# Keeping the first group's turned attention rows in their ring places instead of writing them to DRAM and reading them back

## The chip, the cores and the metric

The kernel runs on one core of a Trainium2 chip. The metric is the device time of one execution in microseconds (us); times of several executions are given with their median. A profile of one execution gives every instruction's start and duration on the engines: TensorE (PE, with its weight loads as PEld), VectorE (DVE), ScalarE (ACT), GpSimd (POOL), and SyncE (SP), whose queue issues nearly all transfers.

## The reference

Three layers on 2304 tokens of 512 channels, in float32. A windowed attention (4 batches of 576 positions, 8 heads of 64, each position sees itself and the 127 before it, with a slope by head); a dense layer with h - tanh(h); and a mixture of 8 experts, in which each token goes to the one expert whose embedding it is most like.

```python
scores = scale * q @ k^T + slope * -(distance), masked to 0 <= distance < 128
attn = softmax(scores) @ v                        # -> x [2304, 512]
h = x @ w_in                                      # w_in [512, 2048]
x = (h - tanh(h)) @ w_out                         # w_out [2048, 512]
e = argmax(norm(x) @ norm(expert_emb)^T / tau);  gate = softmax(...)[e]
out = gate * (relu(x @ w1[e]) @ w2[e])            # w1 [8, 512, 1024], w2 [8, 1024, 512]
```

## The kernel before

The tokens are 18 blocks of 128; two blocks are a group, so there are 9 groups. Products are split into a high and a low part (hi, lo), and three products of the parts make one.

Attention makes a block in four quarters (two heads of scores at a time): scores on TensorE (L463, L469), the bias and the row maximum on VectorE, exp on ScalarE, then the split of the probabilities (L510, L515), a transposing transfer issued by SP (L520, tile pt), the product with the values on TensorE (L551), and a sum into the block's rows xr (L570). xr is a single tile. `x_out` turns it on TensorE (four transposes, L642), copies the high part into the tile xT on ScalarE (L654) and subtracts for the low part on VectorE (L655). xT is a ring of four places, two for a group.

The dense layer takes a group in 8 steps. In a step, two half steps of 12 matmuls each make h from xT and w_in (L695), ScalarE and VectorE make g = h - tanh(h) and its split (L700, L703, L708, tile gl at L712), and four quarters of three matmuls each add g times w_out into the group's accumulators acc (L719), one for each of its two blocks. There is only one pair of accumulators. Half of group 0's weights are not there yet at the start, so the order of visits is: group 0 with the first 4 of the 8 steps (its sums are spilled to DRAM, tile pa, `spill`), group 1 with all 8, group 0 with the other 4, and then groups 2 to 8. The steps are counted through over the visits, from 0 to 71: group 1 has steps 4 to 11, group 0's second visit steps 12 to 15, group 2 begins with step 16.

`route` is the gate of a group: the sums are copied from acc into the tile x2row (group 0: the spilled sums are reloaded into it, L755, and acc added, L759), squared and rooted, split three times (copies L793, subtractions L798, on the engine that the planner chooses), turned by a transfer (L802, x3T), multiplied by the embeddings for the logits (L807), and after the choice TensorE makes the positions (L848 to L851), GpSimd scatters both blocks into the experts' buckets in DRAM (L878). x2row is a single tile, so group 0's reload waits for group 1's scatters. Then the experts run.

What stands where is decided by a planner (`Plan`). Every piece of work is added with its engine (or a choice of engines) and its cost, a due time, and the names that it reads and writes; `order` gives each the engine and the place in that engine's queue at which it would start first by these costs. Each engine runs its queue in order. A piece that goes away can thus change the order of others.

In `x_out` before, the first two blocks are written to DRAM (px) from xr when they are made, and on group 0's second visit read back into xr and turned and split again. The ring places of both visits of group 0 are the same two, since the counter xi goes round by four:

```python
sl = [xi % XR, (xi + 1) % XR]      # XR = 4; visits 0, 1, 0 take places 0-1, 2-3, 0-1
```

Of the kernel before, what the change touches and what calls it, by code (L numbers as in the profile page):

```python
# [10 lines left out]
F32 = mybir.dt.float32  # L11
# [14 lines left out]
DM = H * D  # L26
# [19 lines left out]
N0 = 1  # L46
# [118 lines left out]
class Builder:  # L165
# [461 lines left out]
            P.add({"DVE": 0.5}, recip, due, r=["at"], w=sm)  # L627
            P.add({"DVE": 0.5, "POOL": 0.7}, mul, due, r=["at"] + sm, w=half)

    def x_out(self, P, b, s, due, back=False):  # L630

        nc = self.nc
        v = {}

        def reload(e):
            t = self.xr[b] = self.at.tile([128, DM], F32, tag="xr", name="xr", bufs=1)
            nc.sync.dma_start(out=t, in_=self.px[b])

        def tr(e):
            v["ps"] = self.misc()  # L640
            for k in range(KD):
                nc.tensor.transpose(v["ps"][:, k * 128:(k + 1) * 128], self.xr[b][:, k * 128:(k + 1) * 128],  # L642
                                    self.ident)

        pv = lambda: v["ps"].rearrange("p (k t) -> p k t", k=KD)
        hi, lo = [t[:, s] for t in self.xTs]
        xr, xt = [("xr", m) for m in range(4)], ("xT", s)
        if back:
            P.add({"SP": 0.73}, reload, due - 2, r=["at", ("px", b)], w=xr)
        elif b < 2 * N0:  # L650
            P.add({"SP": 0.73}, lambda e: nc.sync.dma_start(out=self.px[b], in_=self.xr[b]), due, r=["at"] + xr,
                  w=[("px", b)])
        P.add({"PE": 0.43}, tr, due, r=["at", "con"] + xr, w=[xt], take="misc")
        P.add({"ACT": 0.48}, lambda e: self.nc.scalar.copy(out=hi, in_=pv()), due, r=["at"], w=[xt])  # L654
        P.add({"DVE": 0.6}, lambda e: self.nc.vector.tensor_tensor(out=lo, in0=pv(), in1=hi.bitcast(F32),  # L655
                                                                   op=ALU.subtract), due, r=["at"], w=[xt],
              free="misc")
# [588 lines left out]
    def build(self):  # L1246
        tc, nc = self.tc, self.nc
        for n in ("kf", "qf", "vf", "sums", "oh4", "qst", "xr", "acc", "w"):
            setattr(self, n, {})
        self.setup()  # L1250
        dp = self.pool("dr", bufs=1, space=DRAM, tilewait=False)
        self.bucket = dp.tile([ROWS, ROW], F32, name="bucket")
        self.px = dp.tile([2 * N0, 128, DM], F32, name="px")
        self.pa = dp.tile([2 * N0, 128, DM], F32, name="pa")
        self.nw = 0
        P = Plan()
        P.add({"POOL": 0.6}, lambda e: self.small(), 0, w=["small", "cum"])
        self.zero(P)
        self.consts(P)
        self.small_loads(P, -9)  # L1260
        self.emb(P, -9)
        all_f = list(range(FP))
        fa, fb = all_f[:FA], all_f[FA:]
        visits = ([(g, fa) for g in range(N0)] + [(N0, all_f)] + [(g, fb) for g in range(N0)]
                  + [(g, all_f) for g in range(N0 + 1, NG)])

        def weights(fps, due, rate):
            for x, fp in enumerate(fps):
                for kind in "io":
                    for f in (2 * fp, 2 * fp + 1):  # L1270
                        self.weight(P, kind, f, due + x * rate + 1.2 * (kind == "o"))

        weights(fa, -WLEAD, WRATE)
        p, xi, seen = 0, 0, set()
        for g, fps in visits:
            sl = [xi % XR, (xi + 1) % XR]
            xi += 2
            rate = RATE if g <= N0 else 1.0
            for n in range(2):
                b = 2 * g + n  # L1280
                d0 = p - 8 * rate - LEAD + 4 * n * rate
                if g not in seen:
                    for hf in range(2):
                        due = d0 + 2 * hf * rate
                        self.qk_half(P, b, hf, due - QK)
                        if b < NF and hf == 0:
                            self.qk_early(P, b, due - QK - 2)
                            self.v_full(P, b, due)
                        if b >= NF - 1:
                            self.v_half(P, b, hf, due)  # L1290
                        for qq in range(2):
                            self.quarter(P, 4 * b + 2 * hf + qq, due + qq * rate)
                self.x_out(P, b, sl[n], -5 if g in seen else d0 + 4 * rate, g in seen)
            if g == N0:
                weights(fb, p + len(fa) - WLEAD2, WRATE2)
            for fp in fps:
                self.step(P, p, g, fp, sl, fp == fps[0], fp == fps[-1])
                for e in range(E):
                    if p == PAD + e // PADN:
                        self.pad(P, e, p)  # L1300
                p += 1
            if g < N0 and g not in seen:
                self.spill(P, p - 1, g, sl)
            else:
                if g == NG - 1:
                    self.moe2(P, p, lambda: self.route(P, g, sl, p))
                else:
                    self.route(P, g, sl, p + 1)
                if g == NG - 3:
                    self.choose(P, p + 2)  # L1310
            seen.add(g)
        with tc.manual_schedule():
            for fn, e in P.order({"misc": 1}):
                fn(e)
        self.overflow()
        while self.open:
            k = list(self.open)[-1]
            self.close(k)
# [183 lines left out]
```

## Time and profile before

| | |
|---|---|
| median of 3 runs | 810.32 us (808.01 to 810.85) |
| the profiled execution | 813.71 us, its span 812.0 us |
| TensorE busy | 775.1 us (95%), weight loads 684.4 us (84%) |
| VectorE, ScalarE, GpSimd busy | 569.6, 422.0, 227.1 us |
| moved by transfers | 118.90 MB, 146 GB/s on average |
| granted clock of TensorE, mean | 0.992 |

The span runs from the first to the last instruction. A busy share is an average over the whole span; what a stretch is worth is seen in that stretch alone.

### The profile page before, as it was taken

The numbers are of one execution on the slowest core, as the hardware profiler recorded it, in microseconds if no ns is written. First come the engines' busy times: TensorE is split into PE (matmuls) and PEld (weight loads), VectorE is DVE, ScalarE is ACT, GpSimd is POOL, SyncE is SP. The second block draws the span as 40 slices with busy tenths as digits, with TensorE's granted clock in tenths as the row PEclk, the third lists the DMA queues.
The fourth block names the chain that finished last, engine by engine and source line by source line (L and its number), as shares of the span: only waits on it lengthen the run. The fifth ranks groups of instructions, "written<-read, shape, count | busy, mean of one in ns | idle before, by whom it ended". The sixth has DMA issues, their size and how long they took to land. (4 is left out here: it accounts for less than half of the span.)

```text
span 812.0 us, 15246 instructions
## 1 busy us (share of the span) xinstructions
PE 775.1 (95%) x5225; PEld 684.4 (84%) x5225; DVE 569.6 (70%) x1544; ACT 422.0 (52%) x953; POOL 227.1 (28%) x242
## 2 busy tenths in 40 slices
PE   6999999988999998999999999989999999999995
PEld 4688998886888987888988989978879899989894
DVE  5788988968587697788787886776456665756420
ACT  4787866555354455555555643555246554545220
POOL 2113034646253145144242422321100211210210
PEclk9999999999999999999999999999999999999998
DMA  8896079666245335445364442474167666655100
GB/s 306 312 365 229 34 211 271 139 129 136 65 93 132 82 86 117 105 98 119 84 130 112 73 79 53 153 211 143 66 217 231 202 208 202 198 184 184 40 29 30
DMA packets 128264, 118.90 MB, mean 146 GB/s; under 512 B 87973, under 2 KB 92069, under 8 KB 128048
## 3 DMA queue, kind: packets, MB, share of 16 engines
q1 hardware_dynamic: 125152, 108.37, 48.7%
q0 software_dynamic: 3024, 9.46, 3.2%
q8 instruction: 43, 0.70, 0.4%
q14 instruction: 45, 0.37, 0.2%
HBM read 86.84 MB, written 17.08 MB: 128 GB/s over the span
## 5 line engine op out<-in xcount | busy, mean ns | idle before, releaser
L695 PE MATMUL h<-xT,wi 128*128 128x256 f32 x1728 | 225.5, 284 | 0.0
L695 PEld LDWEIGHTS h<-xT,wi 128*128 128x128 f32 x1728 | 217.0, 191 | 5.9 <-issue 1.3
L719 PE MATMUL acc<-wo,gh 128*128 128x512 f32 x576 | 184.8, 402 | 0.3 <-DVE x2row L759 0.3
L719 PE MATMUL acc<-wo,gl 128*128 128x512 f32 x288 | 113.8, 395 | 0.0
L719 PEld LDWEIGHTS acc<-wo,gh 128*128 128x128 f32 x576 | 100.0, 189 | 15.1 <-DVE x2row L759 0.5
L700 ACT ACTIVATE t<-h 128x512 f32<-128x512 f32 x72 | 43.1, 599 | 103.2 <-PE h L695 98.2
L1129 PE MATMUL y<-eo,ge 128*128 128x512 f32 x336 | 88.8, 399 | 0.5 <-ACT ge L1110 0.5
L505 ACT ACTIVATE p<-sc,mx 128x256 f32<-128x256 f32 (+1 forms) x128 | 59.3, 465 | 41.5 <-DVE mx L491 37.7
L1154 POOL DMA_INDIRECT out<-yo,ix x23 | 24.4, 1059 | 188.1 <-ACT yo L1150 39.8
L491 DVE CUSTOM_DVE_ANT_0 sc<-sc,bias 128x256 f32<-128x256 f32 (+1 forms) x144 | 52.6, 371 | 28.5 <-PE sc L469 19.6
L1129 PEld LDWEIGHTS y<-eo,ge 128*128 128x128 f32 x336 | 59.5, 188 | 10.8 <-ACT ge L1110 0.8
L712 DVE TENSOR_TENSOR gl<-t,gh 128x512 fp32r<-128x512 f32 x72 | 64.9, 902 | 4.9 <-ACT gh L708 4.3
L1027 DVE TENSOR_TENSOR eo<-est,eo 128x512 fp32r<-128x512 f32 x61 | 44.9, 738 | 28.8 <-ACT eo L1023 28.1
L719 PEld LDWEIGHTS acc<-wo,gl 128*128 128x128 f32 x288 | 54.4, 189 | 12.6 <-DVE gl L712 0.5
L1023 ACT CAST eo<-est 128x512 fp32r<-128x512 f32 x64 | 39.6, 620 | 37.1 <-PE y L1125 21.3
L1116 DVE SCALAR_TENSOR_TENSOR ge<-he,ge 128x256 fp32r<-128x256 f32 x104 | 28.7, 316 | 41.2 <-ACT ge L1110 41.2
L1094 PEld LDWEIGHTS he<-xA,ei 128*128 128x128 f32 x384 | 54.2, 188 | 2.5
L1094 PE MATMUL he<-xA,ei 128*128 128x288 f32 (+2 forms) x384 | 56.1, 295 | 0.0
L703 DVE TENSOR_TENSOR t<-h,t 128x512 f32<-128x512 f32 x72 | 49.4, 686 | 9.3 <-ACT t L700 9.1
L1110 ACT ACTIVATE ge<-he 128x288 fp32r<-128x288 f32 (+2 forms) x56 | 23.1, 415 | 62.9 <-PE he L1094 58.7
L1094 PEld LDWEIGHTS he<-xT,ei 128*128 128x128 f32 x384 | 53.4, 189 | 2.1
L1094 PE MATMUL he<-xT,ei 128*128 128x288 f32 (+2 forms) x384 | 54.8, 295 | 0.0
(202 smaller groups left out, 1312.1 us busy)
## 6 DMA issues: line engine op xcount, KB each, us to landing
est<-in_w SPq DMA_DIRECT2D x128, 256.0 KB, 3.2
rawi<-in_w_in SPq DMA_DIRECT2D x16, 511.8 KB, 6.9
rawo<-in_w_out SPq DMA_DIRECT2D x16, 511.8 KB, 5.0
stk<-in_k SPq DMA_DIRECT2D x30, 256.0 KB, 2.9
stq<-in_q SPq DMA_DIRECT2D x28, 256.0 KB, 3.1
bucket<-in_c_pad SPq DMA_DIRECT2D x8, 771.0 KB, 6.3
xe<-bucket SPq DMA_DIRECT2D x17, 257.0 KB, 3.5
vst<-in_v SPq DMA_DIRECT2D x30, 128.0 KB, 2.4
```

Source lines behind the costliest of these rows:

```text
L491: nc.vector.tensor_tensor_reduce(out=x, in0=x, in1=self.bias[:, h, c0:c1], scale=-0.125, scalar=mx[:, 1:2] if m else 3.0e38, op0=ALU.add, ...
L505: nc.scalar.activation(out=v["p32"][:, jj * W:(jj + 1) * W], in_=x, func=AF.Exp, scale=-1.0, bias=v["mx"][jj][:, 0:1], accum_out=self.sums ...
L695: nc.tensor.matmul(h3(v["h"], f2), lhsT=w[:, a, k, :], rhs=xT[c][:, :, k, :], start=(k == 0 and n == 0), stop=(k == KD - 1 and n == 2))
L700: nc.scalar.activation(out=v["t"], in_=v["h"].rearrange("p a b -> p (a b)"), func=AF.Tanh)
L703: nc.vector.tensor_tensor(out=v["t"], in0=v["h"].rearrange("p a b -> p (a b)"), in1=v["t"], op=ALU.subtract)
L712: self.eng(e).tensor_tensor(out=v["gl"], in0=v["t"], in1=v["gh"].bitcast(F32), op=ALU.subtract)
L719: nc.tensor.matmul(self.acc[g, t], lhsT=v[a][:, c0:c0 + 128], rhs=self.w["o", fs[f2]][:, c, :], start=(first and f2 == 0 and n == 0), stop ...
L1023: nc.scalar.copy(out=t[:, 0, :], in_=v["x"])
L1027: self.eng(eng).tensor_tensor(out=t[:, 1, :], in0=v["x"], in1=t[:, 0, :].bitcast(F32), op=ALU.subtract)
L1094: nc.tensor.matmul(h[:, 0:N], lhsT=w[:, a, c0:c0 + 128], rhs=xT()[b][:, k, 0:N], start=(k == 0 and n == 0), stop=(k == KD - 1 and n == 2))
L1116: nc.vector.scalar_tensor_tensor(out=g[:, o:o + c1 - c0], in0=hk[f][:, c0:c1], scalar=0.0, in1=g[:, c0:c1].bitcast(F32), op0=ALU.max, op1= ...
L1129: nc.tensor.matmul(y[t], lhsT=gt(f, a)[:, (t - ts[0]) * 128:(t - ts[0] + 1) * 128], rhs=self.w["o", f0 + f][:, b, :], start=(f == 0 and n ...
```

## The change

The blocks of group 0 are turned and split at the first visit only. The write to px, the read back, and the second turning and splitting are gone, and so is the tile px in DRAM. The places of the ring hold what the first visit put there; group 1 between the visits uses the two others.

```diff
-    def x_out(self, P, b, s, due, back=False):
+    def x_out(self, P, b, s, due):
...
-        def reload(e):
-            t = self.xr[b] = self.at.tile([128, DM], F32, tag="xr", name="xr", bufs=1)
-            nc.sync.dma_start(out=t, in_=self.px[b])
...
-        if back:
-            P.add({"SP": 0.73}, reload, due - 2, r=["at", ("px", b)], w=xr)
-        elif b < 2 * N0:
-            P.add({"SP": 0.73}, lambda e: nc.sync.dma_start(out=self.px[b], in_=self.xr[b]), due, r=["at"] + xr,
-                  w=[("px", b)])
...
-        self.px = dp.tile([2 * N0, 128, DM], F32, name="px")
...
-                self.x_out(P, b, sl[n], -5 if g in seen else d0 + 4 * rate, g in seen)
+                if g not in seen:
+                    self.x_out(P, b, sl[n], d0 + 4 * rate)
```

The planner orders everything anew. On all engines its order is again that of before from step 33 on. Lines behind the removed ones have numbers lower by 4 or 9 in the changed kernel (L642 is L638, L719 is L710, L755 is L746, L793 and L798 are L784 and L789, L812 is L803, L878 is L869).

SyncE's queue in the middle of group 1's steps, where the reads back stood. Before:

```order
L319 DMA rawi_874<-in_w_in 128x2047
L637 DMA xr<-px 128x512
L429 DMA vst_910<-in_v 128x256
L359 DMA stk<-in_k 128x512
L359 DMA stq<-in_q 128x512
L429 DMA vst_930<-in_v 128x256
L637 DMA xr<-px 128x512
L429 DMA vst_1007<-in_v 128x256
```

In the changed kernel, at the same place:

```order
L359 DMA stk<-in_k 128x512
L429 DMA vst_865<-in_v 128x256
L319 DMA rawi_881<-in_w_in 128x2047
L359 DMA stq<-in_q 128x512
L429 DMA vst_932<-in_v 128x256
L666 DMA pa<-xspill 128x512 x2
```

The two reads of px are gone, and the last weight load stands behind a load of k.

TensorE's queue at group 2's first sum into acc (step 16), with the scores in front of it. Before:

```order
L469 MATMUL sc_97<-khl,qst_2185 128x256 x2
L469 MATMUL sc_98<-khl,qst_2185 128x256 x2
L719 MATMUL acc_2388<-wo_382,gh 128x512 x2
L719 MATMUL acc_2388<-wo_382,gl 128x512
L719 MATMUL acc_2388<-wo_461,gh 128x512 x2
L719 MATMUL acc_2388<-wo_461,gl 128x512
L719 MATMUL acc_2388<-wo_558,gh 128x512 x2
```

In the changed kernel:

```order
L469 MATMUL sc_97<-khl,qst_2182 128x256 x2
L469 MATMUL sc_98<-khl,qst_2182 128x256 x2
L710 MATMUL acc_2323<-wo_372,gh 128x512 x2
L710 MATMUL acc_2323<-wo_372,gl 128x512
L710 MATMUL acc_2323<-wo_479,gh 128x512 x2
L710 MATMUL acc_2323<-wo_479,gl 128x512
L638 MATMUL misc<-con,xr 128x128 x4
```

Before, the turning of the block's xr stood in front of these scores; now it stands behind the first two sums.

VectorE's queue where the gate of group 1 takes the first block's logits (L812, in the changed kernel L803). Before:

```order
L812 TENSOR_REDUCE lg<-misc 128x8
L703 TENSOR_TENSOR t<-h,t 128x512
L491 ISA sc_98,mx_1947<-sc_98,bias 128x256
L491 ISA mx_1947 128x1
L793 CAST x_90<-xrest 128x512
L570 TENSOR_REDUCE xr<-o 128x128
L712 TENSOR_TENSOR gl<-t,gh 128x512
```

In the changed kernel:

```order
L784 CAST x_90<-x2row 128x512
L803 TENSOR_REDUCE lg<-misc 128x8
L789 TENSOR_TENSOR xrest<-x2row,x_90 128x512
L784 CAST x_90<-xrest 128x512
L789 TENSOR_TENSOR x_90<-xrest,x_90 128x512
L570 TENSOR_REDUCE xr<-o 128x128
```

The second block's whole split (two copies, two subtractions) is VectorE's now; before, one copy was, and both subtractions (L798) were GpSimd's.

## Rows read from the trace of the kernel before

**Rows 1.** Busy time by engine in stretches of us, granted clock, transfers' share, GB/s:

```profile
core 0: us, PE busy (x) PEld busy (x) DVE busy (x) ACT busy (x) POOL busy (x), PEclk, DMA share, GB/s
...
80.00:90.00 10.00, 10.00 (x64) 8.93 (x64) 9.97 (x18) 9.17 (x17) 1.81 (x2) 1.00 0.19 67
...
182.00:184.00 2.00, 1.98 (x13) 1.56 (x9) 1.31 (x6) 0.93 (x2) 1.80 (x3) 0.50 0.72 223
...
204.00:206.00 2.00, 2.00 (x7) 1.62 (x6) 0.84 (x2) 0.00 (x0) 0.00 (x0) 0.53 0.00 0
```

**Rows 2.** Waits of TensorE, 40 to 300 us: total, times, longest:

```profile
PE o L551 <- DMA pt<-ph: 3.0, 3, 2.2
PE misc L807 <- DMA x3T<-x: 2.3, 3, 1.7
```

**Rows 3.** TensorE's timeline: start, duration, instruction, in brackets the idle before:

```profile
134.90 0.39 PE L719 MATMUL acc<-wo,gl 128*128 128x512 f32 x1
...
152.72 0.46 PE L807 MATMUL misc<-en,x3T 128*128 128x24 bf16 x12
...
163.30 0.46 PE L807 MATMUL misc<-en,x3T 128*128 128x24 bf16 x12
...
167.09 0.18 PE L848 MATMUL misc<-oh,tri 128*128 128x8 bf16 x1
...
187.53 0.73 PE L719 MATMUL acc<-wo,gh 128*128 128x512 f32 x2 [0.29 <-DVE x2row L759]
...
201.74 0.46 PE L807 MATMUL misc<-en,x3T 128*128 128x24 bf16 x12 [1.71 <-DMA x3T<-x]
```

**Rows 4.** TensorE's timeline in group 1's steps:

```profile
104.17 0.40 PE L469 MATMUL sc<-khl,qst 128*128 128x256 f32 x2
104.40 0.62 PE L719 MATMUL acc<-wo,gh 128*128 128x512 f32 x2
...
105.79 0.62 PE L719 MATMUL acc<-wo,gh 128*128 128x512 f32 x2
...
106.48 3.04 PE L695 MATMUL h<-xT,wi 128*128 128x256 f32 x24
109.35 0.63 PE L719 MATMUL acc<-wo,gh 128*128 128x512 f32 x2
...
110.05 0.73 PE L551 MATMUL o<-vt,pt 128*128 128x192 bf16 x8
110.59 0.70 PE L719 MATMUL acc<-wo,gh 128*128 128x512 f32 x2
```

**Rows 5.** TensorE's timeline, the second reloaded block being turned:

```profile
80.53 0.60 PE L642 MATMUL misc<-con,xr 128*128 128x128 f32 x4
80.89 0.71 PE L719 MATMUL acc<-wo,gh 128*128 128x512 f32 x2
```

**Rows 6.** Waits of SyncE's queue, 0 to 60 us: total, times, longest:

```profile
SPq L651 <- DVE xr L581: 12.4, 2, 7.8
```

**Rows 7.** Timelines of GpSimd, SyncE and VectorE; for the reload KB and us to landing:

```profile
168.84 1.36 POOL L878 DMA_INDIRECT bucket<-x2row,ix  x1 [1.35 <-DVE ix L871]
...
175.47 0.99 POOL L878 DMA_INDIRECT bucket<-x2row,ix  x1 [0.16 <-issue]
...
181.64 0.33 SPq L755 DMA_DIRECT2D x2row<-pa  x1
...
x2row<-pa SPq DMA_DIRECT2D x2, 256.0 KB, 3.0
...
186.20 0.68 DVE L655 TENSOR_TENSOR xT<-misc,xT 128x512 fp32r<-128x512 f32 x1
186.80 0.68 DVE L759 TENSOR_TENSOR x2row<-x2row,acc 128x512 f32<-128x512 f32 x1
```

**Rows 8.** Timelines of VectorE and GpSimd in the gate of group 1:

```profile
144.92 0.42 DVE L793 CAST x<-xrest 128x512 bf16<-128x512 f32 x1
...
154.30 1.28 POOL L369 TENSOR_TENSOR khl<-stk,khl 64x512 fp32r<-64x512 f32 x1 [0.34 <-DVE t L703]
...
154.32 1.55 DVE L793 CAST x<-xrest 128x512 bf16<-128x512 f32 x1
```

## The prediction

> **What bounds the kernel now.** I read first the stretches by engine, then who waited for whom on TensorE, then the timeline of the stretch in which TensorE loses most.
>
> Where nothing is wrong TensorE is the bound: between 80 and 90 us it is busy for 10.00 of 10.00 us, although VectorE is busy for 9.97 us beside it [rows 1]. So a piece of VectorE or ScalarE work that goes away there is worth nothing unless TensorE waits for it, and TensorE work that goes away is worth what it occupies. From 40 to 300 us TensorE's named waits are few: 3.0 us for turned probabilities and 2.3 us for the turned token rows of the gate [rows 2]. The larger part of both stands in one place, behind 179 us, where the rows show a half clock too: 0.50 of full speed from 182 to 184 us, and 0.53 from 204 to 206 us [rows 1], that is 1.2 GHz in place of 2.4 after TensorE had idled.
>
> That place is one long chain. Group 1's last product into its accumulator starts at 134.90 us and is over at about 135.1 (the distance of such products is taken below); then come the gate of group 1, which needs TensorE at 152.72 and 163.30 us (logits of its two blocks) and at 167.09 us (the positions), and then the scatter of its rows, the reload of group 0's spilled sums into the tile that the scatter has just freed, and the addition. Only then is group 0's accumulator free, and group 2's first sum starts at 187.53 us, released by that addition [rows 3]. From 135.1 to 187.5 are 52.4 us.
>
> **How much of the 52.4 us is TensorE's own work.** Starts of neighbours give what each piece occupies [rows 4]: two scores 104.40 - 104.17 = 0.23 us, a quarter of the second product 106.48 - 105.79 = 0.69, two half steps of the first 109.35 - 106.48 = 2.87, thus 1.435 each, one product with the values 110.59 - 110.05 = 0.54. Turning four blocks of xr takes 80.89 - 80.53 = 0.36 [rows 5]. Logits and positions are taken as 0.3 and 0.14, an estimate below the 0.46 and 0.18 of their rows [rows 3], since their instructions overlap as well. In the order of before there stand in this stretch 16 half steps, 16 quarters, 9 products with values, 18 scores, 2 turnings: 23.0 + 11.0 + 4.9 + 4.1 + 0.7 + 0.8 = 44.5 us. So 7.9 us of the 52.4 are waiting and half clock.
>
> **The change part by part.**
>
> *Removed from TensorE:* two turnings of xr (the second at 80.53 us), where TensorE is full: 2 x 0.36 = 0.7 us. The upper bound is their rows' own duration, 2 x 0.60 = 1.2 us [rows 5]; the lower is nothing, if the weight loads beside them set the pace. I take 0.7. The Trainium skill, TensorE: Matmul & The Clock Gate, Part 4, puts one turned 128x128 block at about 275 ns within a kernel; eight of them would be 2.2 us as an estimate from that page, and the sum below would be 1.5 us lower. The rows decide against it: four blocks are followed by the next product after 0.36 us, because they overlap.
>
> *Removed from ScalarE and VectorE:* two copies and two subtractions (a subtraction is 0.68 us [rows 7]), at a time when TensorE never waits: nothing. Had TensorE been paced by VectorE there, it would be up to 1.4 us.
>
> *Removed from SyncE's queue:* two writes and two reads of 256 KB, and with the writes a wait: the queue stood 12.4 us, up to 7.8 at once, in front of them until xr was there, with weight loads behind it [rows 6]. TensorE's waits behind 40 us list no weights [rows 2], so nothing; what could be had before 40 us, which those rows leave out, is left to the bounds.
>
> *Moved:* the planner's order is the same again from step 33 on, on all engines. Before that, three things change in the stretch of 52.4 us. The gate's splits of group 1 move from GpSimd to VectorE (three of four subtractions). The logits stand earlier on TensorE: 4 half steps behind the last product and not 6. And between the positions and group 2's first sum TensorE has more to do: 8 half steps, 3 quarters, 3 products with values, 8 scores against 7, 0, 3, 10 and a turning: 11.5 + 2.1 + 1.6 + 1.8 + 0.1 = 17.1 us of cover against 14.5. In all the changed stretch holds 42.6 us of work, and 1.9 us (two products with values, two scores, a turning) stand behind it instead.
>
> **What the stretch will take.** Two ends. If nothing waits in it: 42.6 + 1.9 - 52.4 = -7.9 us. If the chain takes its 52.4 us regardless: +1.9 us. Between them I go by the links. To the first logits there are 13.3 us of work, where the chain took 152.72 - 135.1 = 17.6; but there the work on TensorE was 16.9, so TensorE and not the chain set that time, and subtractions of 0.68 us on VectorE replace ones queued on GpSimd: I take a wait of 1.5 us (0 to 4.3). The second logits have 8.2 us of cover, against 10.6 before: 0.5 us. From the positions on, the chain's rows are [rows 7]: first scatter at 168.84, second at 175.47, the reload issued at 181.64, 14.55 us behind the positions; it lands 3.0 us later, and the addition takes 0.68: 18.2 us against 17.1 us of cover, so 1.1 us of wait. In before the addition came later still, at 186.80, since on VectorE it stood behind the subtraction of a turned xr (186.20), for which TensorE, at half clock, was late; in the changed order this turning stands behind the first sums, so this hold is gone. Waits of 1.5 + 0.5 + 1.1 = 3.1, and 0.5 for a little half clock, make 3.6 us in place of 7.9. The stretch is worth -7.9 + 3.6 = -4.3 us.
>
> What is late next is the turned gate input of group 0, 1.7 us at 201.74 [rows 2, 3]: its cover behind the first sum stays about the same, so I leave that wait and the half clock behind it (2 us at 0.53 cost 0.9 [rows 1]) as they are; they could go, or come twice, for 2.6 us either way.
>
> *Sum:* -0.7 - 4.3 = -5.0 us. The profiled execution took 813.71 us around a span of 812.0, so it would take 808.7; it lies 3.4 us above the median of the runs, 810.32, so on the median's scale 805.3 us.
>
> **The rivals.**
>
> *The chain keeps its length.* Only TensorE's orders differ, and the gate, the scatters and the reload are as slow as before. For it: the two scatters are 6.6 us apart although each is about a microsecond on GpSimd, because splits and subtractions stand between them [rows 7], and the new order has three such instructions there, not two. Against it: the splits leave GpSimd. It gives -0.7 + 1.9 = +1.2, so 811.5 us; a chain a little quicker gives anything between that and the forecast. All of these down to 806.3 are within 0.5%, which is about what a measurement of this kernel tells from no change (4.05 us).
>
> *The chain gets longer: VectorE's splits collide with GpSimd's work.* The same cast of 128x512 took 0.42 us at 144.92 us and 1.55 us at 154.32, and a GpSimd subtraction ran from 154.30 to 155.58 [rows 8]; so an instruction of VectorE can be held until one of GpSimd is over, 1.1 us each. Twelve of VectorE's instructions lie on the changed chain (two squares, six splits, the scalings and the choice); if each were held so, its links would be 13.6 us longer than TensorE's work: 42.6 + 13.6 + 1.9 - 52.4 - 0.7 = +5.0, so 815.3 us. It decides the sign from about eleven holds, which give the +4.05 us that count as slower. Against it: most rows of VectorE beside it show no hold, and the old chain held some too. The Trainium skill, SBUF — State Buffer, SBUF: two separate sides, says that the two engines share a port pair that one of them locks for a whole instruction, for VectorE instructions with two SBUF inputs among others; by that rule the subtractions are open to it, and the pair of rows agrees in kind.
>
> *The transfers were hidden and the rest is noise:* -0.7 us, 809.6; this is inside the first rival's span and counted with it.
>
> **How the numbers follow.** Forecast, faster by more than 0.5%: 0.52. The chain as long as before or less shortened, and all that is within 0.5%: 0.40. Slower: 0.08. Predicted 805.3 us. The low end is the stretch without any wait, -0.7 - 7.9 = -8.6, thus 801.7, put at 801.0 for part of the wait at 201.74; the high end is the chain unshortened, 811.5. For the likeliest case alone: 801.0 to 806.3.
>
> **What would show it.** Right: four loads and stores fewer on SyncE, no turning of xr between 75 and 85 us; group 1's last product to group 2's first sum in 45 to 48 us and not 52.4; a wait of under 2 us for the addition; a clock that does not fall, or falls for less, behind it. Wrong: the same 52 us with the wait at other places (at the first logits above all), casts of 1.2 us and more in the gate's splits on VectorE, or a new wait for turned probabilities before 135 us, where transposes now stand behind the padding writes on SyncE.

## The result, and the profile after

The changed kernel takes 799.96 us (median of 4 runs, 799.12 to 801.11), the kernel before 809.2 in the same comparison (808.01 to 810.85): ratio 0.9882, 95% interval 0.9858 to 0.9906. The forecast was 805.3 with a range from 801.0 to 811.5. The direction was right; the gain is 9.2 us where 5.0 were forecast, and the time lies 1.0 us below the range. The profiled execution took 800.38 us, its span 798.6, so the two profiled executions differ by 13.3 us; the medians count.

Stretches of the changed kernel by engine, in answer to [rows 1] (columns as there):

```profile
80.00:90.00 10.00, 10.00 (x65) 9.07 (x64) 8.93 (x15) 8.64 (x16) 0.00 (x0) 1.00 0.39 133
182.00:184.00 2.00, 2.00 (x10) 1.61 (x10) 2.00 (x6) 1.52 (x4) 0.53 (x1) 1.00 0.73 138
204.00:206.00 2.00, 2.00 (x20) 1.59 (x17) 1.83 (x11) 1.25 (x4) 0.23 (x1) 1.00 0.06 11
```

TensorE is as full as before between 80 and 90 us. The half clock, 1.2 GHz, that [rows 1] show from 182 and from 204 us is gone: 1.00 in both, and in every stretch of 4 us from 40 to 300 us.

Waits of TensorE from 40 to 300 us (total, times, longest), in answer to [rows 2]:

```profile
PE o L551 <- DMA pt<-ph: 3.6, 4, 1.0
PE o L551 <- DVE gl L703: 0.9, 1, 0.9
PE misc L798 <- DMA x3T<-x: 0.9, 2, 0.7
PE acc L710 <- DVE x2row L750: 0.7, 1, 0.7
```

No wait is longer than 1.01 us; the waits for turned probabilities are more in total than before (3.6 us against 3.0), but the long ones are gone. TensorE's timeline through the long stretch, in answer to [rows 3]:

```profile
131.12 0.40 PE L710 MATMUL acc<-wo,gl 128*128 128x512 f32 x1
...
145.64 0.46 PE L798 MATMUL misc<-en,x3T 128*128 128x24 bf16 x12 [0.68 <-DMA x3T<-x]
...
154.50 0.46 PE L798 MATMUL misc<-en,x3T 128*128 128x24 bf16 x12
155.67 0.53 PE L551 MATMUL o<-vt,pt 128*128 128x192 bf16 x5 [0.71 <-DMA pt<-ph]
...
177.09 0.73 PE L551 MATMUL o<-vt,pt 128*128 128x192 bf16 x8 [1.01 <-DMA pt<-ph]
...
179.06 0.74 PE L710 MATMUL acc<-wo,gh 128*128 128x512 f32 x2 [0.72 <-DVE x2row L750]
```

From the end of group 1's last product (131.12 plus 0.23, the distance of such products) to group 2's first sum are 47.7 us, where [rows 3] gave 52.4.

A second place has nothing to do with that stretch. At step 36, in the part of the program where the planner's order is that of before on all engines, TensorE's timeline of before has

```profile
309.68 0.73 PE L551 MATMUL o<-vt,pt 128*128 128x192 bf16 x8 [2.28 <-DMA pt<-ph]
```

and that of the changed kernel

```profile
297.99 0.73 PE L551 MATMUL o<-vt,pt 128*128 128x192 bf16 x8 [1.01 <-DMA pt<-ph]
```

The same product waits 1.27 us less for the same transposing transfer. To follow this over the kernel I use the start of each step's tanh on ScalarE (L700, in the changed kernel L691). In the two profiled executions the changed kernel is ahead by 3.8 us at step 0 already, gains 0.9 from step 0 to step 9 (62.99 us before, 62.08 after), 6.7 from step 11 to 21 (84.47 and 77.80), and then 1.3 at steps 35 to 37, 1.4 from 42 to 43 and 0.6 from 52 to 53. In between it also loses: 0.6 from step 9 to 11, 0.3 from 21 to 35 and 1.1 from 37 to 42.

### The profile page after: what moved, and what is told of

The parts are those of the page before. It is cut to its first block, busy times and chain, and to the rows that moved or that the text cites. A ratio compares the mean times of both kernels' runs of the same rounds, so it can differ in the third digit from the quotient of the medians.

```text
span 798.6 us, 15190 instructions
## 1 busy us (share of the span) xinstructions
PE 765.5 (96%) x5217; PEld 677.4 (85%) x5217; DVE 571.3 (72%) x1543; ACT 419.5 (53%) x950; POOL 228.0 (29%) x242
## 4 chain that ended last, share of the span: by engine, by line
PE 62%; DMA 13%; DVE 10%; issue 9%; ACT 3%; POOL 2%; SPq 0%; POOLq 0%; DVEq 0%; ACTq 0%
PE h L686 18%; PE acc L710 17%; PE he L1085 8%; PE y L1120 7%; DMA pt<-ph 4%; DMA est<-in_w 3%; PE o L551 3%; DMA out<-yo,ix 3%; PE y L1116 2%; PE sc L469 2%; DMA x3T<-x 2%; DVE gl L703 1%; DMA vst<-in_v 1%; DVE sc L491 1%; PE misc L1042 1%
## 5 line engine op out<-in xcount | busy, mean ns | idle before, releaser
L710 PE MATMUL acc<-wo,gh 128*128 128x512 f32 x576 | 184.1, 401 | 0.7 <-DVE x2row L750 0.7
L710 PE MATMUL acc<-wo,gl 128*128 128x512 f32 x288 | 113.2, 393 | 0.1
L710 PEld LDWEIGHTS acc<-wo,gh 128*128 128x128 f32 x576 | 99.5, 189 | 15.3 <-DVE x2row L750 0.9
L691 ACT ACTIVATE t<-h 128x512 f32<-128x512 f32 x72 | 43.1, 598 | 100.9 <-PE h L686 91.9
L1145 POOL DMA_INDIRECT out<-yo,ix x23 | 22.1, 961 | 192.1 <-ACT yo L1141 39.3
L710 PEld LDWEIGHTS acc<-wo,gl 128*128 128x128 f32 x288 | 54.1, 188 | 12.6 <-DVE gl L703 0.6
L515 POOL TENSOR_TENSOR ph<-p,ph 128x512 f16<-128x512 f32 (+1 forms) x30 | 36.8, 1225 | 65.9 <-ACT ph L510 45.8
```

The costliest lines, as they stand in the source:

```text
L515: self.eng(e).tensor_tensor(out=ph[:, 2 * W:4 * W], in0=v["p32"][:, 0:2 * W], in1=ph[:, 0:2 * W], op=ALU.subtract)
L691: nc.scalar.activation(out=v["t"], in_=v["h"].rearrange("p a b -> p (a b)"), func=AF.Tanh)
L710: nc.tensor.matmul(self.acc[g, t], lhsT=v[a][:, c0:c0 + 128], rhs=self.w["o", fs[f2]][:, c, :], start=(first and f2 == 0 and n == 0), stop ...
```

## The experiments

**The theories at the start.** *A*: the gain is the new order in the long stretch, with 0.7 to 0.9 us of turnings. *B*: the writes that wait in SyncE's queue cost the 3.8 us ahead of step 0. *C*: those 3.8 us are of that one profiled execution. *D*: the removed work gives all and the new order nothing. Every time below is compared with the kernel before as it ran on the same chip; its medians there were 807.9 to 809.4 us.

**The order of before, with the work removed by parts.** The pieces stay in the planner's list at their old cost, and some do nothing:

```diff
+        none = lambda e: None
-            P.add({"SP": 0.73}, reload, due - 2, r=["at", ("px", b)], w=xr)
+            P.add({"SP": 0.73}, none, due - 2, r=["at", ("px", b)], w=xr)
...
-        P.add({"PE": 0.43}, tr, due, r=["at", "con"] + xr, w=[xt], take="misc")
+        P.add({"PE": 0.43}, none if back else tr, due, r=["at", "con"] + xr, w=[xt], take="misc")
```

and so for the write, the copy and the subtraction. The second run puts the write back, the third the write and the read.

> All the removed work is gone (two writes, two reads, two turnings, two splittings), but every other instruction stands where it stood before: the pieces are still planned at their old cost and then do nothing. Theory A, the gain is the new order in the 52.4-us stretch: only the two turnings count here, 0.7 to 0.8 us less than before (about 808.4), the stretch from group 1's last product to group 2's first sum stays at 52 us, and a half clock stays behind it. Theory B, the writes that wait in SyncE's queue cost 3.75 us in the first 43 us: 4.5 us less (about 804.7), tanh of step 0 near 43 us and TensorE's rows at full speed from about 17 us on. Theory D, the removed work itself gives all and the order nothing: about 800.

> As the run with the order of before and all removed work gone, but the two writes to DRAM are still made, with their wait in SyncE's queue. Theory A: no difference to that run, 808.4. Theory B: the writes cost their 3.75 us here, 808.4, while the run without them is at 804.7, and TensorE's rows come to full speed only at about 31 us. Theory D: between 800 and 808.

> The order of before with writes and reads kept; only the second turnings and splittings are gone (the reads land and nobody takes them). Theory A: -0.7 to -0.8 us, 808.4, as in the two other runs. Theory B: 808.4 as well, with the run without writes at 804.7. If turnings cost eight times 0.275 us, 2.2 us less than before: 807.0.

Measured, with the kernel before at 808.67: all removed work gone 803.44 (ratio 0.9943, 0.9917 to 0.9969); writes kept 805.0 (0.9956, 0.9928 to 0.9984); all transfers kept 804.45 (0.9955, 0.9933 to 0.9977). The three intervals lie over each other, so the transfers and their place in SyncE's queue are worth nothing that this measurement can tell, and B and D fall. But 4.2 us with nothing gone except two turnings and splittings is more than A allows. From step 0 to 9 that run gains the 0.9 us of the turnings (62.09; of this 0.8 is lost again by step 11). It gains again at steps 35 to 37 (14.92 us against 16.37), 42 to 43 (7.50 and 8.66) and 52 to 53 (6.97 and 7.53): 3.2 us, 220 us and more behind the removed work, in an unchanged order.

**The kernel before once more.**

> The kernel before once more, for a second profile of its first 43 us. Theory C, that the late full speed (rows of doubled duration up to 31 us) is of that one profiled execution: rows at full speed from 17 to 20 us here, tanh of step 0 near 43 us, and a time near 808 to 810. Theory B: doubled durations up to about 31 us again and tanh of step 0 at 46 to 47 us.

It took 812.36 us, with the first tanh at 45.03 us. The eight-product sums of the first blocks in TensorE's timeline of this execution:

```profile
22.98 1.16 PE L540 MATMUL of<-vf,ptf 128*128 128x128 f32 x8
25.32 1.16 PE L540 MATMUL of<-vf,ptf 128*128 128x128 f32 x8
30.43 1.86 PE L540 MATMUL of<-vf,ptf 128*128 128x128 f32 x8
```

In the first profile of before the row of 26.30 us had 2.07 and that of 30.31 us 1.86. So such rows are short early, and long again, in one and the same kernel. The granted clock goes with it, in the same execution (columns as in [rows 1]: 1.00, 0.84 and 0.74):

```profile
24.00:28.00 4.00, 2.91 (x22) 2.18 (x20) 1.07 (x3) 1.50 (x5) 1.34 (x2) 1.00 1.00 365
28.00:32.00 4.00, 2.65 (x12) 2.16 (x13) 3.97 (x17) 3.77 (x10) 0.00 (x0) 0.84 1.03 413
32.00:36.00 4.00, 4.00 (x22) 2.88 (x22) 2.04 (x7) 2.82 (x8) 0.67 (x1) 0.74 0.90 363
```

Over all profiles of this study the first tanh starts between 41.2 and 47.1 us (the changed order: 42.5 to 46.2), and the records of the granted clock in the traces sort them. In six profiles the first record of full clock begins between 17.0 and 19.0 us and no fall follows before 40 us: first tanh at 41.2 to 43.6 us. In six it begins between 16.8 and 19.8 us, or at 13.8, but the clock falls to half once before 35 us: 43.6 to 45.4. In six it begins only between 29.0 and 31.8 us: 45.1 to 47.1. Both orders stand in each of the three. In the pair of the result it begins at 31.81 us before and at 17.18 us in the changed kernel. C holds: the 3.8 us ahead of step 0 are no effect of the change, but of the clock in that execution.

**What moved at steps 36, 43 and 53.** The transfers' view of before from 304 to 310 us, in 40 slices of 0.15 us:

```profile
GB/s 0 0 3 152 225 213 217 203 208 212 224 215 200 172 205 188 217 195 268 215 56 0 0 0 0 9 9 10 10 10 239 295 289 294 273 273 82 14 14 178
...
q8 instruction: 1, 0.02, 1.0%
```

Two transposing transfers were issued at 303.27 (x3T) and 304.79 (pt). The traffic runs at about 200 GB/s, nearly stops at about 307.1 us for 1.35 us (nine slices), and goes on. Just ahead of the gap, between 306.75 and 306.90 us, one packet of 16 KB went over the queue named "q8 instruction". That queue carries 0.70 MB in 43 such packets in the whole kernel, while TensorE's instructions are some 10,960 (5,481 products in the program, of which the trace has 5,225, and a weight load for each): one code load of TensorE for about every 256 instructions. Eight transposes fewer are 16 instructions fewer, so every later load falls 16 instructions later in the program, about 1 us on the mean (an estimate, 812 us over 10,960 instructions; at step 36 it is 3.4 to 4.0 us). This is theory *L*: a code load that falls on a transposing transfer holds it up, and the change moved the loads. It can be tried without touching the work, by small products at TensorE's start, where it has nothing to do until its first loads are there at 5.6 us (40 of them take 1.2 us):

```diff
+        ps = self.misc()
+        for _ in range(8):
+            nc.tensor.matmul(ps[:, 0:E], lhsT=self.ones, rhs=self.oh[:, 0, :], start=True, stop=True)
```

> The changed kernel once more, in more executions. Theory A (the new order in the stretch is worth about 4 us beside the removed work): 799 to 800, some 3.5 to 4.5 us below the run with the order of before and all removed work gone (803.4). Theory D (the removed work gives all): 803, as that run.

> The changed kernel with eight small products (8 columns each, into a bank that nobody reads) at TensorE's start, where it waits for its first loads. TensorE then has as many instructions as before ahead of everything, so its code loads, one for every 256 instructions, fall at the same places of the program as before the change. Theory L, three waits of 2.3, 1.1 and 0.4 us at steps 36, 43 and 53 of before came from a code load that lands while a transposing transfer runs: they come back, about 3 us more than the changed kernel (803). Rival, the waits have another cause: no difference to the changed kernel (800).

The changed kernel took 800.81 (0.9910, 0.9883 to 0.9936, the kernel before at 807.94), and with eight products 802.43 (0.9928, 0.9903 to 0.9954). The intervals overlap, so the times alone don't decide; the profiles do. With eight products the load of step 36 lies between 297.75 and 297.90 us, 2 us behind the issue of pt at 295.79, and the traffic from 295 to 301 us has the gap again:

```profile
GB/s 0 0 14 166 220 217 213 207 212 207 215 220 203 171 205 251 203 191 300 137 55 10 10 10 12 5 9 10 9 10 133 292 287 364 382 451 232 382 314 382
...
q8 instruction: 1, 0.02, 1.1%
```

and the wait is back in TensorE's timeline to within a hundredth (before: 2.28):

```profile
300.65 0.73 PE L554 MATMUL o<-vt,pt 128*128 128x192 bf16 x8 [2.27 <-DMA pt<-ph]
```

Without them the load lies at 299.1 us, behind the transfers. Their traffic, from 292.5 to 298.5 us, then drops for two slices, 0.3 us, and the row is

```profile
GB/s 0 0 0 0 0 2 147 227 217 213 205 205 205 217 218 218 176 201 233 212 215 212 184 61 14 237 287 290 50 116 348 382 335 300 96 410 369 191 55 109
...
297.32 0.73 PE L551 MATMUL o<-vt,pt 128*128 128x192 bf16 x8 [0.97 <-DMA pt<-ph]
```

All 18 profiles of this study agree at step 36: the three with a load 2.0 us behind the issue of pt have 2.28, 2.28 and 2.27 us there, the fifteen others 0.85 to 1.11. From 52 to 53 the 0.7 us came back too (7.70 against 6.97); at step 43 nothing did (7.39 and 7.48), against what L had expected. The load there lies 2.72 us behind the issue of pt, where it was 2.69 in before, at the end of the transfers' traffic in both; in before a last packet of 4 bytes came 0.8 us behind the rest, in this run none did.

> The kernel before, with nothing removed and 40 such small products at TensorE's start: its code loads fall about 5.6 us earlier in the program, clear of the transposing transfers of steps 36, 43 and 53. Theory L: the three waits go, about 3 us less than before (805.6), unless the loads meet other transfers; the profile shows which. Rival: 808.7, or a little more for the 40 products.

With nothing removed, 40 idle products make the kernel before 6.5 us faster: 801.41 (0.9922, 0.9898 to 0.9945). That is more than the three waits. They are gone (steps 35 to 37: 14.51 us, 42 to 43: 7.47, 52 to 53: 6.96), and so is one more, that of 2.17 us for pt at 181.61 us in the long stretch, where a load had come at 177.4, 2 us behind the issue at 175.34. At that place the run has

```profile
178.20 0.73 PE L554 MATMUL o<-vt,pt 128*128 128x192 bf16 x8 [1.01 <-DMA pt<-ph]
```

Over the ten profiles in the order of before this wait is 1.9 to 3.4 us where a load falls 1.4 to 2.0 us behind that issue (six), and 1.0 to 1.8 us where none does (four). The same holds away from these places. Of the transfers of pt issued between 100 and 540 us in all 18 profiles whose landing is on record, 213 have no load from 3 us ahead of their issue to 6 us behind it, and land 3.1 us after it (median; one in ten takes more than 3.9). Twenty have a load 1 to 2 us behind their issue: 4.5 us, and 3.9 at the least.

**Engines of the gate's splits.** In the changed kernel's order, the four subtractions of group 1 run on GpSimd:

```diff
-            P.add(sub, lambda e, t=t: rest(e, t, 0), ...
+            P.add(sub, lambda e, t=t: rest("POOL" if g == N0 else e, t, 0), ...
```

> The changed kernel in its own order, with all four subtractions of group 1's gate on GpSimd as before; only the engine of three instructions changes. If the stretch is shorter because the splits are VectorE's: waits at the first and second logits of 2 to 4 us in all, about 803. If it is shorter because of what stands where on TensorE: within 0.7 us of the changed kernel.

802.02 us (0.9926, 0.9899 to 0.9953), an interval that overlaps the changed kernel's; steps 11 to 21 take 77.30 us against 76.57 and 77.80 in the two profiles of the changed kernel, and the stretch itself 48.2 against 47.5 and 47.7. The splits' engine is worth 0.5 to 0.7 us in the stretch by these single profiles, and nothing that the times can tell; the rest of the stretch's gain is what stands where on TensorE.

**Pairs at equal shift.** Since the loads' places alone move either kernel by several us, I compared the two kernels at more shifts.

> The kernel before with 8 small products at TensorE's start (16 instructions: code loads about 1.1 us earlier in the program). Theory L: the load at step 36 still falls on the transposing transfers, that at step 43 no more: 1 to 2 us less than before, 806 to 807. Rival: no difference, 808.

> The kernel before with 24 small products at TensorE's start (48 instructions: code loads about 3.4 us earlier). Theory L: the time lies where the places of the loads put it, between that with 40 products (801.4) and that with none (808); the load of the long stretch (177.3 us before) falls ahead of the transposing transfer that it met, so the wait of 2.2 us there goes to about 1. Rival: no difference, 808.

> The changed kernel with 24 small products. Its distance to the kernel before with as many is the change's worth at another place of the code loads. Theory A (removed turnings and the new order are a gain of their own): 3 to 5 us less than the kernel before with 24. Theory L alone (the change does nothing but move the code loads, and takes out 0.9 us of turnings): within 1 us of it.

> The changed kernel with 40 small products. Theory A: 3 to 5 us less than the kernel before with 40 (801.4), thus 796.5 to 798.5, which would beat both kernels. Theory L alone: 800 to 801.

> The kernel before with 120 small products at TensorE's start: 240 instructions more, which puts a code load every 256 instructions where 16 fewer would put it. Theory L: the waits at steps 36, 43 and 53 are as in the runs that had the second turnings removed (1.0, 0, 0), with nothing removed: about 3 us less than before. Rival: 808 to 809 as before.

> The changed kernel with 120 small products; with the kernel before at as many it makes a pair at equal shift. Theory A: 3 to 5 us less than that. Theory L alone: within 1 us.

> The kernel before with 72 small products, a pair at another shift. By theory L between 801 and 808, wherever the loads fall.

> The changed kernel with 72 small products. Theory A: on the mean over all pairs (0, 8, 24, 40, 72, 120) 3 to 5 us less than before at equal shift, with single pairs from about +1 to -9. Theory L alone: a mean within 1 us of nothing.

Medians against the kernel before on the same chip, ratio with interval, and TensorE's waits for transposing transfers (pt and x3T) from 100 to 540 us in the profiled execution:

| small products | before | its waits | changed | its waits | changed minus before |
|---|---|---|---|---|---|
| 0 | 0 | 12.1 | -9.2 and -7.1 us, 0.9882 and 0.9910 (above) | 7.9 and 6.7 | -8.2 |
| 8 | -2.7 us, 0.9967 (0.9940 to 0.9994) | 6.2 | -5.5 us, 0.9928 (0.9903 to 0.9954) | 9.4 | -2.8 |
| 24 | -4.8 us, 0.9936 (0.9911 to 0.9960) | 6.2 | -7.5 us, 0.9900 (0.9866 to 0.9933) | 6.1 | -2.7 |
| 40 | -6.5 us, 0.9922 (0.9898 to 0.9945) | 5.6 | -4.2 us, 0.9935 (0.9910 to 0.9961) | 10.0 | +2.3 |
| 72 | +0.8 us, 0.9996 (0.9967 to 1.0024) | 10.8 | -8.2 us, 0.9876 (0.9839 to 0.9914) | 4.7 | -8.9 |
| 120 | +0.5 us, 0.9981 (0.9952 to 1.0009) | 10.5 | -7.2 us, 0.9882 (0.9847 to 0.9918) | 6.1 | -7.7 |

The waits of the first row are these two rows of before (the sum of 7.8 and 4.3 is 12.1),

```profile
PE o L551 <- DMA pt<-ph: 7.8, 8, 2.3
PE misc L807 <- DMA x3T<-x: 4.3, 6, 1.7
```

and these of the kernel before with 40 products:

```profile
PE o L554 <- DMA pt<-ph: 4.1, 5, 1.0
PE misc L810 <- DMA x3T<-x: 1.5, 4, 0.9
```

Two things are to be seen. In this table the waits for transposing transfers, taken from one execution each, go with the time: before is fast where they are near 6 us and slow where they are 10 to 12, and the changed kernel is slowest where its own are 9 to 10. The runs that left out the second turnings fit less well: waits of 7.9, 12.1 and 10.4 us in their profiles, at 5.2, 3.7 and 4.2 us less than before. And the change's worth runs from -8.9 to +2.3 us; its mean over the six shifts is -28.0 / 6 = -4.7 us, with a standard error of 1.8 (the spread of the six, 4.4, over the root of six). By the ratios, which do not follow the medians exactly, the mean is -5.2.

Six pairs leave a 95% interval of -9.3 to -0.1 us for that mean, so by the times alone A is likely and L alone, a mean within 1 us of nothing, is not quite excluded. The profiles of the same pairs tell more, since they show where the change acts. Steps 11 to 21 are shorter in every pair, by 0.9 to 7.0 us, 4.7 on the mean (standard error 0.9); from step 33 to 71, where the order is the same, the pairs go from -5.4 to +1.3 us, -1.5 on the mean (standard error 1.1; with no products, each kernel's two profiles are averaged). So the new order has a worth of its own, and behind it the loads give or take. That all of the pair's excess over the mean is the loads is argued from this and not shown piece by piece.

The expectations for single pairs missed: A's 3 to 5 us stood against 2.7 with 24 products and 7.7 with 120. With 8 products L had the load of step 36 still fall on the transfers of before; it came 1.6 us ahead of the issue of pt, and the wait was 0.98 us. With 24 the wait in the long stretch was 1.40 us, where about 1 was expected, and before with 72 took 808.8, just outside L's 801 to 808.

With 120 products, 240 instructions, the loads of before come to the places that 16 fewer instructions give them. The three waits did as L said (steps 35 to 37: 15.09 us, 42 to 43: 7.39, 52 to 53: 6.97), but the time, 808.52, didn't fall as the expectation had it, since the loads met other transfers. One of them, in TensorE's timeline, with a load at 217.3 us and the issue at 217.47, where SyncE's issuing instruction itself took 2.54 us against 1.24 without a load (in the six profiles of that order with no load within 1 us of the issue the same row waits 0 to 0.4 us; of the four with one, three wait 1.3 to 2.2 and one not at all):

```profile
223.25 0.73 PE L554 MATMUL o<-vt,pt 128*128 128x192 bf16 x8 [1.41 <-DMA pt<-ph]
```

The changed kernel with 40 is the opposite case, against what A had expected of it. Loads at 156.2 and 279.7 us fall on transposing transfers,

```profile
158.13 0.46 PE L801 MATMUL misc<-en,x3T 128*128 128x24 bf16 x12 [1.62 <-DMA x3T<-x]
...
282.47 0.73 PE L554 MATMUL o<-vt,pt 128*128 128x192 bf16 x8 [1.61 <-DMA pt<-ph]
```

and the first is followed by a granted clock of 0.73 from 160 to 164 us. No run beats the changed kernel beyond its interval; 72 products (0.9876) are the lowest ratio, but the interval holds 0.9882.

## Why the prediction was wrong in size, point by point

**The turnings (0.7 us, between 0 and 1.2): right.** Steps 0 to 9 are 0.9 us shorter in the changed kernel and in all three runs that leave out the second turning, also where the transfers stay; 0.6 to 0.8 us of it are lost again between steps 9 and 11 in these four profiles.

**ScalarE, VectorE and SyncE's queue (nothing): right.** The runs with writes or with all transfers kept can't be told from the run without, although the wait of [rows 6] is gone from SyncE's queue and no block is turned between 75 and 85 us any more. The early gain that only the pair of profiles shows belongs to the execution and its clock.

**The long stretch (-4.3 us): right on the mean over shifts, but not by its terms, and too small for the pair at hand.** Over the six shifts the stretch takes 52.2 us before (50.8 to 53.9) and 47.6 changed (46.9 to 49.7). With the 1.9 us of work that moved behind it, this is -2.7. But steps 11 to 21, which hold the stretch and what follows, shrink by 4.7 on the mean (81.6 to 76.9), 6.4 in the pairs without products. The difference was given to "what is late next": the wait of 1.7 us at 201.74 and the half clock behind it were left as they are, "could go, or come twice". They went. In the repeat profile of before that wait is 0.47 us and the clock full behind it, so a part of this belonged to the one execution that the prediction read. Nine of the ten profiles in the order of before show the clock below 0.98 of full speed in a stretch of 4 us between 176 and 194 us, and one of the eight in the changed order shows it fall anywhere from 40 to 300. Link by link: 1.5 us forecast at the first logits, 0.68 measured; 0.5 and none at the second; 1.1 and 0.72 for the addition; and two waits for turned probabilities, 0.71 and 1.01, that the forecast did not have. The sum of the waits is right so, 3.1 us; TensorE's own work was put too low. Before, the named waits in the 52.4 us are 3.9 us (2.17 of them at 181.61), and the half clock there cost 1.7 (0.50 from 182 to 184, 0.65 from 184 to 186), so 46.8 us were work, and not 44.5; in the changed stretch 47.7 less 3.1 are 44.6, and not 42.6. So the stretch had 5.6 us to win and not 7.9, and what it missed of the forecast came back behind it, where the half clock went.

**The step that failed** is "The planner's order is the same again from step 33 on, on all engines", from which the sum took nothing for all that follows, and by which [rows 2] could be read as waits of the kernel's own links. An equal order is not an equal program: 16 fewer TensorE instructions moved 43 code loads. In the pair of kernels at hand this took the three waits of steps 36, 43 and 53 away, 3.2 us in the run that kept the transfers, and put others in. From step 33 to 71, for which the sum had nothing, the changed kernel was 2.4 us faster in the profiles of the result and 8.4 in the two repeats, and over the six shifts anything from 5.4 faster to 1.3 slower. The wait of 2.17 us for turned probabilities at 181.61 in the long stretch was in part a load as well: it is 1.01 us in before with 40 products and in the changed kernel. The range lacked this term, several us of either sign. Taken out by the pairs, the change is worth 4.7 us (standard error 1.8), and the sum had 5.0; with TensorE's work mis-sized and a clock that was not counted on, that agreement is in part luck.

**The rivals.** That the chain keeps its length fell with the 47.7 us. That VectorE's splits collide with GpSimd did not decide: one subtraction of the changed gate took 1.60 us on VectorE, at 149.00 us, beside a GpSimd instruction from 148.88 to 150.06, where its neighbours took 0.68 and 0.69. So such a hold was there, but giving the subtractions back to GpSimd gains nothing.

Left open: why a load of 16 KB stops a transposing transfer for more than a microsecond, when other traffic passes beside loads (381 GB/s between 299.0 and 299.5 us in the repeat of the changed kernel, with the load at 299.13); and why the full clock is granted at 17 us in some executions and only at 30 in others.

## What to carry to other kernels

Before a gain or a loss of a per cent is put down to a change, move the code loads and look again: a few instructions without use at the start of the busiest engine shift them, and the mean over several shifts is the change's own worth. In the trace, look at the instruction queue's packets beside each transposing transfer that lands late, above all where a wait differs although the order is the same. In a kernel whose time varies by this much, look at the granted clock at its start as well. And an order that is equal behind some point doesn't promise equal time there when the number of instructions ahead of it has changed.

## What the runs showed of the hardware that was not expected

- One code load of 16 KB, 2.0 us behind the issue of the second of a pair of transposing transfers, nearly stopped their traffic for 1.35 us, where 0.3 is the pause without it, and made TensorE wait about 1.3 us longer (2.27 and 2.28 us in three profiles, in two orders, against 0.85 to 1.11 in fifteen). The Trainium skill, Runtime: NRT & Kernel Launch, Instruction fetch mechanics, says that instructions come in blocks of 16 KiB, 256 each, and that the cost of crossing a block is mostly hidden. The trace agrees on the size (0.70 MB in 43 loads); on the cost it differs where a transposing transfer is under way, and there the measurement decides.
- Up to 6.5 us, 0.8% of this kernel, came from 40 small products alone whose result nobody reads.
- In the first 35 us rows of equal work had 1.16 or 1.86 to 2.07 us in executions of one kernel, and some 3 us of the start hang on it. The column of the granted clock shows 1.00 for the stretches from 24 to 32 us of the first profile of before, with rows of 1.86 and 2.07 us in them; but the trace's clock records begin only at 31.81 us there, so this 1.00 is no reading. Where the records reach, the rows go with them: in the repeat, 1.16 us at full clock and 1.86 in the row at 30.43, in which the clock fell.
